# FNet and MLP mixer on one core: the first tile's mean in halves, the second tile loaded behind the third chunk of weights, and the products of the first two tiles alternated

## The chip, the core and the metric

The kernel runs on one core of a Trainium2 chip. A core has five engines with a queue of instructions each: TensorE (matrix products; PE in the profile, its weight loads PEld), VectorE (DVE), ScalarE (ACT), GpSimd (POOL) and SyncE (SP, which here issues transfers). They run side by side and wait for one another by semaphores. The metric is the device time of one execution in microseconds; the figure for a kernel is the median of several executions without the profiler.

## The reference

`x` is 2048 tokens of 512 features, float32. The reference normalizes, mixes by a discrete Fourier transform over features and tokens, and gates the result by an MLP:

```python
xn = layernorm(x)                         # over the features, eps 1e-5, no scale or shift
a  = xn @ dft_hid_re.T                    # 2048 x 512
b  = xn @ dft_hid_im.T
s  = dft_seq_re @ a - dft_seq_im @ b      # real part of the transform over the tokens
h  = gelu(layernorm(xn) @ w1 + b1)        # 512 -> 1792, tanh form
g  = silu(h @ w2 + b2)                    # 1792 -> 512
out = x + s * g
```

## The kernel before

Every operand of a product is kept as two float32 parts, a rounded one (high, made by ScalarE) and what is left (low, made by VectorE as the difference), and a product is three products of TensorE: high by high, low by high, high by low. Below, `hl2` means: high part of the tile, low part of the weights, chunk 2 of the 512 features.

The stages follow one another on TensorE: the transform over the features (`pd`, lines 361 and 376, then `q` for the last tokens), the MLP (`h`, `m`), and the transform over the tokens (`px`, `pz`, `pw`). The tokens go in 16 tiles of 128. The first four tiles are loaded as rows, centred and transposed by TensorE; the other tiles come from a transposed copy of `x` in memory and are centred with a row of means. The factors 1/sqrt(variance) are applied later, where a product leaves PSUM.

The order of the instructions is written out by hand: each engine runs its instructions in the order in which the program's lines issue them, and waits where an operand is not there yet. The change touches the head of the kernel, the first 25 us or so. Its pieces:

- `x_load(i)` (line 211) and `load_w` (line 221) issue transfers on SP's queue, 256 KB each: one tile of `x`, or one of the eight chunks of feature weights `wt[m, k]` (`m` 0 the real part, 1 the imaginary, `k` the chunk of 128 features). Chunk `n` here is `m * 4 + k`.
- `first_mean(i)` (line 249), `first_centre(i)` (line 256), `first_var(i)` (line 262): mean, centring and variance of a row tile. Tile 0's mean and variance come from VectorE's `bn_stats` (line 118) and `bn_aggr` (line 119), the others' from sums that ScalarE accumulates as it copies or squares (lines 252 and 263).
- `first_transpose(i)` (line 265): four transposes by TensorE, then the split into high (ScalarE, line 64) and low part (VectorE, line 65). Tile 0 goes in two halves.
- `round_w(n)` and `rest_w(n)` (lines 297 and 302): high part of a chunk by ScalarE (line 300), low part by VectorE (line 83).
- `first_mm` (line 366): tile 0's products with both halves of the weights, tile 1's transposes among them. `dft_mm(i, m)` (line 355): twelve products of tile `i`; it can issue something (`mid`) before its n-th product.
- `idle_mm` (line 192): products of zeros at the start and before the first real product.
- `m_pack` and `m_turn` (lines 309 and 314): means of tiles 4 to 7 packed as columns, transposed by TensorE, stored, and loaded back by SP as a row over all partitions. `xt_centre` and `xt_make` then centre and split these tiles.

The order of the head, as written in the kernel before:

```python
x_load(0); load_w(0, 0); load_w(0, 1); load_w(1, 0); x_load(1); load_w(1, 1); x_load(2); x_load(3)
```

so x0, chunks 0 to 5, x1, chunks 6 and 7, x2, x3. Chunk 0 is split, tile 0 transposed, chunks 1 to 5 split, tile 1 centred, chunks 6 and 7 split. The products: all twelve of tile 0 with the real part, six with the imaginary one, tile 1's transposes, the other six, then tile 1 with the real part (tile 2's transposes among them), tile 1 with the imaginary part, the turn of the row of means, tile 2.

Of the kernel before, what the change touches and what calls it, by code (L numbers as in the profile page):

```python
# [8 lines left out]
F32 = mybir.dt.float32  # L9
# [3 lines left out]
AF = mybir.ActivationFunctionType  # L13
ALU = mybir.AluOpType

P = 128
# [6 lines left out]
def fnet_mixer_kernel(ctx: ExitStack, tc: tile.TileContext, x, xT, ct, wt, w1, w2, b1, b2, out):  # L23
    nc = tc.nc
    S, D = x.shape
    assert D == W
    NS = S // P
    NK = D // P
# [8 lines left out]
    small = ctx.enter_context(tc.tile_pool(name="small", bufs=4))  # L37
# [18 lines left out]
    def bank(name):  # L56
        return psum.tile([P, W], F32, tag="ps", name=name)

    def room(name):
        return lp.tile([P, 2, W], F32, tag="l", name=name)  # L60
# [41 lines left out]
    mv1 = consts.tile([P, NS, 2], F32, name="mv1")  # L102
# [13 lines left out]
    def stats(mv, t, i):  # L116
        st = small.tile([P, 6], F32, tag="st", name="st")
        nc.vector.bn_stats(st, t)
        nc.vector.bn_aggr(mv[:, i, :], st)
# [21 lines left out]
    def first_factors():  # L141
        v = small.tile([P, 2 * HB], F32, tag="v", name="v")
        inner(v[:, :HB], mv1[:, :HB, 1], 1.0)
        outer(v[:, HB:], mv1[:, :HB, 1], 1.0)
        rsqrt(rr[:, :2 * HB], v, 2 * HB)
        nc.vector.tensor_scalar(nr1, rr[:, :HB], -1.0, None, op0=ALU.mult)
# [45 lines left out]
    def idle_mm(n):  # L192
        for q in range(n):
            nc.tensor.matmul(idle_ps, idle[:, :P], idle, start=True, stop=True)  # L194
# [3 lines left out]
    xs = {}  # L198
# [9 lines left out]
    def parts(i):  # L208
        return 1 if i else 2

    def x_load(i):
        if i % 2 == 0:
            x_two[i // 2] = guest(f"x{i}")
        xs[i] = x_two[i // 2][:, i % 2, :]
        nc.sync.dma_start(out=xs[i], in_=x[tok(i) * P:(tok(i) + 1) * P, :])

    raw_w = []
    room_w = {}


    def load_w(m, k2):
        t = room(f"rw{m}{k2}")
        for k in (2 * k2, 2 * k2 + 1):
            nc.sync.dma_start(out=t[:, k % 2, :], in_=wt[m, k])
            raw_w.append(t[:, k % 2, :])
        room_w[m, k2] = t

    warm = small.tile([P, 1], F32, tag="warm", name="warm")
    nc.vector.memset(warm, 0.0)
# [1 line left out]
    nc.scalar.dma_start(out=touched[:P // 8].rearrange("p (n w) -> p n w", w=4),  # L231
                        in_=wt[:, :, 0:P:8, 0:4].rearrange("m k p w -> p (m k) w"))
    x_load(0)
    for k2 in range(NK // 2):
        load_w(0, k2)
    load_w(1, 0)
    x_load(1)
    load_w(1, 1)
    x_load(2)
    x_load(3)  # L240
    a_d = [dram.tile([2, P, D], F32, name=f"a_d{i}") for i in range(NS // 2)]
# [4 lines left out]
    xt = {}  # L246
    xc = {}

    def first_mean(i):
        xc[i] = plain(f"xc{i}")  # L250
        if i:
            nc.scalar.activation(xc[i], xs[i], AF.Copy, scale=1.0 / D, accum_out=mv1[:, i, 0:1])
        else:
            stats(mv1, xs[i], i)

    def first_centre(i):
        n = D // parts(i)
        for q in range(parts(i)):
            nc.vector.tensor_scalar(xc[i][:, q * n:(q + 1) * n], xs[i][:, q * n:(q + 1) * n], mv1[:, i, 0:1], None,
                                    op0=ALU.subtract)  # L260

    def first_var(i):
        nc.scalar.activation(xs[i], xc[i], AF.Square, scale=D ** -0.5, accum_out=mv1[:, i, 1:2])

    def first_transpose(i):
        t = operand(f"xt{i}")
        hi, lo = t[:, 0, :], t[:, 1, :]
        n = D // parts(i)
        for q in range(parts(i)):
            pt = bank(f"pt{i}{q}")  # L270
            for k in range(NK // parts(i)):
                nc.tensor.transpose(pt[:, k * P:(k + 1) * P], xc[i][:, q * n + k * P:q * n + (k + 1) * P], ident)
            split_into(hi[:, q * n:(q + 1) * n], lo[:, q * n:(q + 1) * n], pt[:, :n])
        for k in range(NK):
            xt[i, k] = (hi[:, k * P:(k + 1) * P], lo[:, k * P:(k + 1) * P])
# [19 lines left out]
    weights = [None] * (2 * NK)  # L295

    def round_w(n):
        t = operand(f"W{n}")
        weights[n] = (t[:, 0, :], t[:, 1, :])
        nc.scalar.activation(weights[n][0], raw_w[n], AF.Copy)  # L300

    def rest_w(n):
        rest(weights[n], raw_w[n])
# [10 lines left out]
    def m_turn():  # L314
        ps = bank("rpm1")
        nc.tensor.transpose(ps[:NC, :P], row_st["m1"], ident)
        sb = small.tile([NC, P], F32, tag="rt", bufs=1, name="rtm1")
        nc.scalar.activation(sb, ps[:NC, :P], AF.Copy)
        d = dram.tile([COPIES, W], F32, name="rdm1")
        nc.scalar.dma_start(out=d.rearrange("r (b p) -> b r p", p=P),  # L320
                            in_=sb[:, None, :].broadcast_to([NC, COPIES, P]))
        t = guest("rowm1_0")
        n = P // COPIES
        for r in range(COPIES):
            nc.sync.dma_start(out=t[r * n:(r + 1) * n, 0, :], in_=d[r].partition_broadcast(n))
        mrow[1] = t[:, 0, :]
# [9 lines left out]
    def act_stats(i):  # L336
        if not squares:
            squares.append(guest("squares"))
        t, = squares
        c = i % NC  # L340
        nc.scalar.activation(t[:, 0, :], xs[i], AF.Copy, scale=-1.0 / D, accum_out=nm[:, NC + c:NC + c + 1])
        nc.scalar.activation(t[:, 1, :], xs[i], AF.Square, bias=nm[:, NC + c:NC + c + 1], accum_out=sq[:, c:c + 1])
# [9 lines left out]

    dacc, e_two = {}, {}

    def dft_mm(i, m, mid=None, at=2 * NK):
        acc = bank(f"pd{i}_{m}")
        terms = [(0, 0, k) for k in range(NK)] + [(1, 0, k) for k in range(NK)] + [(0, 1, k) for k in range(NK)]
        for n, (px, pw, k) in enumerate(terms):
            if mid and n == at:
                mid()  # L360
            nc.tensor.matmul(acc, xt[i, k][px], weights[m * NK + k][pw], start=n == 0, stop=n == len(terms) - 1)  # L361
        dacc[i, m] = acc

    def first_mm(mid):
        for m in range(2):
            dacc[0, m] = bank(f"pd0_{m}")
        seen = [0, 0]
        for m, what in ((0, "hh0 hl0 lh0 hh1 lh1 hl1 hh2 lh2 hl2 hh3 lh3 hl3"), (1, "hh0 lh0 hh1 lh1 hl0 hl1"),  # L370
                        (None, ""), (1, "hh2 lh2 hh3 lh3 hl2 hl3")):
            if m is None:
                mid()
            for o in what.split():
                px, pw, k = "hl".index(o[0]), "hl".index(o[1]), int(o[2])
                nc.tensor.matmul(dacc[0, m], xt[0, k][px], weights[m * NK + k][pw], start=seen[m] == 0,  # L376
                                 stop=seen[m] == 3 * NK - 1)
                seen[m] += 1

    def dft_at(i, m):  # L380
        return (b_d if m else a_d)[tok(i) // 2][tok(i) % 2]
# [14 lines left out]
    def store():  # L396
        dst, e = stores.pop(0)
        nc.sync.dma_start(out=dst, in_=e)

    first_mean(0)  # L400
    first_centre(0)
    round_w(0)
    rest_w(0)
    first_transpose(0)
    for n in (1, 2, 3, 4, 5):
        round_w(n)
        rest_w(n)
    first_mean(1)
    first_centre(1)
    for n in (6, 7):  # L410
        round_w(n)
        rest_w(n)
    for q in range(NC):
        x_load(NC + q)
    xt_load(1)
    for q in (12, 13, 8, 9):
        x_load(q)

    idle_mm(1)
    first_mm(lambda: first_transpose(1))  # L420
    first_mean(2)
    first_var(1)
    first_centre(2)
    stats(mv1, xs[NC], NC)
    stats(mv1, xs[NC + 1], NC + 1)
    dft_mm(1, 0, mid=lambda: first_transpose(2))
    first_mean(3)
    first_var(2)
    first_centre(3)
    first_var(3)  # L430
    stats(mv1, xs[NC + 2], NC + 2)
    stats(mv1, xs[NC + 3], NC + 3)
    m_pack()
    dft_mm(1, 1)
    m_turn()
    for q in (14, 15, 10, 11):
        x_load(q)
    for q in (12, 13):
        act_stats(q)
    first_factors()  # L440
    for q in (8, 9):
        stats(mv1, xs[q], q)
    dft_mm(2, 0, mid=lambda: first_transpose(3))
    dft_out(0, 0)
    dft_out(0, 1)
    dft_out(1, 0)
# [137 lines left out]
    for i in range(3, HB):  # L584
        if i == 3:
            xt_prepare(1)
            for q in (14, 15):
                act_stats(q)
            for q in (10, 11):
                stats(mv1, xs[q], q)  # L590
            neg_means(2)
            neg_means(0)
        if i == 4:
            second_factors()
        if i == 5:
            a_sums()
            last_factors()
        if i == 6:
            for b in (2, 3):
                for k2 in range(2):  # L600
                    y_centre(b, k2)
        if i == 7:
            y_scale(0, 2)
            y_round("11", 1)
            y_scale(1, 2)
            y_round("21", 1)
            y_rest("11", 1)
            y_rest("21", 1)
        dft_mm(i, 0, mid=turn_r if i == 5 else None, at=2)
        if i == 5:  # L610
            rrow = [None] * 2 + row_load("R", 2, 2)
        dft_out(i - 1, 1)
        if i == 4:
            row_st["n"] = nm
            rows_turn("n")
            mrow[2], mrow[3] = row_load("n", 2)
        dft_mm(i, 1)
        dft_out(i, 0)
# [640 lines left out]
```

## Time and profile before

| what | value |
|---|---|
| median of 3 executions | 667.26 us (667.09 to 667.33) |
| profiled execution: whole time | 668.27 us |
| profiled execution: span from first to last instruction | 666.5 us |
| TensorE busy | 661.4 us, 99% of the span, 2926 products and transposes |
| VectorE busy | 542.5 us, 81% |
| ScalarE busy | 358.3 us, 54% |
| granted TensorE clock | 1.000 over the span |

The profile is one execution with the profiler on. A row of its timeline gives the start and the duration in microseconds from the start of the span, the engine, the line of the kernel, the operation, the names written and read (`pd<-W,xt`), the shapes, and how many like instructions are merged (`x8`); the brackets at the end give how long the engine had stood idle before and what ended that wait. `DMA` there means a transfer that landed. The chain that ended last follows the work back from the last instruction, each time to what released it. Names: `x` row tiles, `xc` centred, `pt` transposed in PSUM, `xt` split; `rw` raw chunks of weights, `W` split; `pd` products.

### The profile page before, as it was taken

To read this page: it belongs to the slowest core of one execution; us is meant where nothing else is said; L and a number is where in the kernel's file an instruction comes from. 1 tells how busy PE (TensorE), PEld (TensorE's weight loads), DVE (VectorE), ACT (ScalarE), POOL (GpSimd) and SP (SyncE) were. 2 spreads that over 40 slices of the span, in tenths; PEclk is the share of its full clock that TensorE was granted. 3 is DMA by queue.
4 is the path that set the end of the run, shared out by engine and by line. 5 is a ranking of instruction groups with operands and counts; after the bars stand their busy time and mean duration, and the time that the engine had idled before them with its cause. 6 is when DMAs were issued, how large, how long until landed. Compare 5 with 4: busy or idle time off the path is not lost.

```text
span 666.5 us, 8218 instructions
## 1 busy us (share of the span) xinstructions
PE 661.4 (99%) x2926; PEld 544.6 (82%) x2926; DVE 542.5 (81%) x590; ACT 358.3 (54%) x407; POOL 50.7 (8%) x84
## 2 busy tenths in 40 slices
PE   9999999999999999999999999999999999999997
PEld 5888888888888888888888888888888888888886
DVE  6889878867777866988979998739878299998986
ACT  6836647554456655555455544446545454746540
POOL 0002000321212100000000000000000001210100
PEclk9999999999999999999999999999999999999999
DMA  8689360787889999797799996416545448996983
GB/s 312 221 287 236 107 241 4 299 312 288 328 307 351 416 415 357 270 392 275 297 389 409 358 326 236 158 40 212 184 152 139 128 125 263 304 258 243 309 255 137
DMA packets 70821, 172.29 MB, mean 258 GB/s; under 512 B 6864, under 2 KB 21756, under 8 KB 70780
## 3 DMA queue, kind: packets, MB, share of 16 engines
q1 hardware_dynamic: 58528, 131.88, 56.2%
q0 software_dynamic: 12032, 39.86, 19.1%
q8 instruction: 23, 0.38, 0.2%
q14 instruction: 18, 0.15, 0.1%
q10 hardware_dynamic: 220, 0.02, 0.0%
HBM read 121.38 MB, written 50.35 MB: 258 GB/s over the span
## 4 chain that ended last, share of the span: by engine, by line
PE 99%; DVE 0%; issue 0%
PE pz L873 20%; PE px L873 18%; PE ma L873 11%; PE hy L688 11%; PE mb L873 9%; PE pd L361 6%; PE hz L688 6%; PE pw L873 5%; PE qy L568 3%; PE hx L688 3%; PE px L1194 2%; PE pw L1194 2%; PE qz L568 2%; PE pd L376 1%; PE qx L568 1%; PE idle_ps L194 1%
## 5 line engine op out<-in xcount | busy, mean ns | idle before, releaser
L979 DVE TENSOR_TENSOR c<-c,c 128x1024 f32<-128x1024 f32 x32 | 38.9, 1217 | 4.8 <-DMA c<-ct 4.8
L83 DVE TENSOR_TENSOR w1l<-w1r,w1h 128x1792 fp32r<-128x1792 f32 x7 | 14.2, 2026 | 21.6 <-ACT w1h L475 21.6
L693 ACT ACTIVATE hc<-hc,b_t 128x1024 f32<-128x1024 f32 (+1 forms) x18 | 17.3, 960 | 25.2 <-DVE hc L733 22.6
L65 DVE TENSOR_TENSOR R_b1l<-c,R_b1h 128x1024 fp32r<-128x1024 f32 x16 | 19.5, 1221 | 13.0 <-ACT R_b1h L64 9.7
L64 ACT ACTIVATE R_s3h<-c 128x1024 fp32r<-128x1024 f32 x16 | 17.0, 1061 | 23.7 <-DVE c L979 12.3
L873 PE MATMUL pw<-R_s1h,L 128*128 128x512 f32 x96 | 29.7, 389 | 0.0
L64 ACT ACTIVATE R_b2h<-c 128x1024 fp32r<-128x1024 f32 x16 | 16.9, 1058 | 21.2 <-DVE c L984 16.7
L65 DVE TENSOR_TENSOR R_s2l<-c,R_s2h 128x1024 fp32r<-128x1024 f32 x16 | 19.5, 1221 | 8.6 <-PE pz L873 8.6
L64 ACT ACTIVATE R_s2h<-c 128x1024 fp32r<-128x1024 f32 x16 | 17.0, 1061 | 16.7 <-PE px L873 9.3
L65 DVE TENSOR_TENSOR R_s3l<-c,R_s3h 128x1024 fp32r<-128x1024 f32 x16 | 19.5, 1218 | 4.0 <-PE pz L873 4.0
L64 ACT ACTIVATE R_s1h<-c 128x1024 fp32r<-128x1024 f32 x16 | 16.4, 1050 | 11.4 <-DVE c L990 11.4
L987 POOL DMA_DIRECT2D c<-ct x8 | 7.0, 873 | 200.6 <-DVE c L984 162.9
L64 ACT ACTIVATE R_b1h<-c 128x1024 fp32r<-128x1024 f32 x16 | 16.7, 1053 | 9.5 <-PE px L873 4.4
L64 ACT ACTIVATE R_a1h<-c 128x1024 fp32r<-128x1024 f32 x16 | 16.9, 1054 | 8.9 <-PE pz L873 7.2
L873 PEld LDWEIGHTS pw<-R_s1h,L 128*128 128x128 f32 x96 | 18.0, 188 | 3.7
L65 DVE TENSOR_TENSOR R_b2l<-c,R_b2h 128x1024 fp32r<-128x1024 f32 x16 | 19.4, 1218 | 1.5 <-PE px L873 1.5
L65 DVE TENSOR_TENSOR R_a1l<-c,R_a1h 128x1024 fp32r<-128x1024 f32 x16 | 19.5, 1219 | 1.3 <-PE px L873 1.1
L65 DVE TENSOR_TENSOR R_s4l<-c,R_s4h 128x1024 fp32r<-128x1024 f32 x16 | 19.5, 1217 | 0.7 <-PE px L873 0.7
L984 DVE TENSOR_TENSOR c<-c,c 128x1024 f32<-128x1024 f32 x16 | 19.6, 1223 | 0.4
L64 ACT ACTIVATE R_s4h<-c 128x1024 fp32r<-128x1024 f32 x16 | 16.8, 1051 | 5.3 <-PE pz L873 5.0
L65 DVE TENSOR_TENSOR R_s1l<-c,R_s1h 128x1024 fp32r<-128x1024 f32 x16 | 18.8, 1219 | 0.4 <-ACT R_s1h L64 0.2
L64 ACT ACTIVATE w2h<-w 128x1024 fp32r<-128x1024 f32 (+1 forms) x14 | 13.2, 944 | 10.6 <-DVE w L801 3.9
(954 smaller groups left out, 2226.4 us busy)
## 6 DMA issues: line engine op xcount, KB each, us to landing
c<-ct SPq DMA_DIRECT2D x68, 512.0 KB, 5.1
m<-h_d SPq DMA_DIRECT2D x48, 512.0 KB, 6.8
h_d<-ht POOLq DMA_DIRECT2D x21, 512.0 KB, 5.9
s_d<-sa SPq DMA_DIRECT2D x32, 256.0 KB, 4.0
la<-s_d SPq DMA_DIRECT2D x32, 256.0 KB, 6.6
h_d<-hc POOLq DMA_DIRECT2D x13, 512.0 KB, 3.8
x<-x SPq DMA_DIRECT2D x16, 256.0 KB, 5.4
sa<-a_d SPq DMA_DIRECT2D x8, 512.0 KB, 5.7
```

Of the source, the lines that this page charges most:

```text
L64: nc.scalar.activation(hi, src, AF.Copy)
L65: nc.vector.tensor_sub(lo, src, hi.bitcast(F32))
L83: nc.vector.tensor_sub(hi_lo[1], src, hi_lo[0].bitcast(F32))
L361: nc.tensor.matmul(acc, xt[i, k][px], weights[m * NK + k][pw], start=n == 0, stop=n == len(terms) - 1)
L568: nc.tensor.matmul(qx[key, c], a, w, start=p in (1, 5, 2) and n == 0, stop=p in (2, 3, 4) and n == len(terms) - 1, skip_group_check=True)
L688: nc.tensor.matmul(acc[:, tau, :], w[:, W1_AT[p], k * P:(k + 1) * P], r[:, k, :], start=p in (1, 5, 2) and i == 0, stop=p in (2, 3, 4) and ...
L693: nc.scalar.activation(dst, src, AF.Gelu_apprx_tanh, bias=b1_t[:, row:row + 1])
L873: nc.tensor.matmul(acc[k][:, tau, :], a, c[:, tau, :], start=first and i == 0, stop=last and i == len(terms) - 1, skip_group_check=True)
L979: nc.vector.tensor_sub(t, t, raw)
L984: nc.vector.tensor_add(raw, raw, t)
L987: nc.gpsimd.dma_start(out=t, in_=ct[1, 1, n], accum_op=ALU.add)
L1194: nc.tensor.matmul(acc[KEY[name]][k][:, tau, cols], a[k], c[:, tau, cols], start=False, stop=last and u == us[-1] and i == 2, skip_group_c ...
```

## The change

The first tile's mean is taken in halves: ScalarE sums the first 256 columns while it copies them (with the factor 1/512), VectorE sums the other 256 with a reduction and scales the sum; centring subtracts both half means in one instruction. Tile 0's variance is no more a by-product and is made by ScalarE, in the same way as the other tiles', and a small addition puts the mean together for later use. On SP's queue x1 stands behind chunk 2 instead of chunk 5. ScalarE and VectorE split chunks 1 and 2, then make tile 1's mean and centre it, then split chunks 3 and 4; chunks 5 to 7 come behind tile 1's transposes. The products of tiles 0 and 1 are issued in turns. The turn of the row of means, and what is issued with it, moves two products further, into tile 2's.

```diff
-    for k2 in range(NK // 2):
-        load_w(0, k2)
-    load_w(1, 0)
+    for n in range(3):
+        load_w(n)
     x_load(1)
-    load_w(1, 1)
+    for n in range(3, 2 * NK):
+        load_w(n)
     x_load(2)
     x_load(3)
...
+    half_means = [small.tile([P, 1], F32, tag=f"hm{q}", bufs=1, name=f"hm{q}") for q in range(2)]
...
         if i:
             nc.scalar.activation(xc[i], xs[i], AF.Copy, scale=1.0 / D, accum_out=mv1[:, i, 0:1])
-        else:
-            stats(mv1, xs[i], i)
+            return
+        n = D // 2
+        nc.scalar.activation(xc[i][:, :n], xs[i][:, :n], AF.Copy, scale=1.0 / D, accum_out=half_means[0])
+        nc.vector.reduce_sum(half_means[1], xs[i][:, n:], axis=mybir.AxisListType.X)
+        nc.vector.tensor_scalar(half_means[1], half_means[1], 1.0 / D, None, op0=ALU.mult)
...
+        for q in range(2):
+            nc.vector.tensor_scalar(xc[i][:, q * n:(q + 1) * n], xs[i][:, q * n:(q + 1) * n], half_means[0],
+                                    half_means[1], op0=ALU.subtract, op1=ALU.subtract)
...
     first_mean(0)
     first_centre(0)
-    round_w(0)
-    rest_w(0)
+    make_w(0)
     first_transpose(0)
-    for n in (1, 2, 3, 4, 5):
-        round_w(n)
-        rest_w(n)
+    idle_mm(1)
+    make_w(1, 2)
     first_mean(1)
     first_centre(1)
-    for n in (6, 7):
-        round_w(n)
-        rest_w(n)
+    make_w(3, 4)
+    first_mm(0, 0, "hh0 hl0 lh0 hh1 lh1 hl1 hh2 lh2 hl2 hh3 lh3")
+    first_transpose(1)
+    first_mm(0, 0, "hl3")
+    make_w(5, 6, 7)
...
-    idle_mm(1)
-    first_mm(lambda: first_transpose(1))
+    first_mm(0, 1, "hh0 lh0 hl0")
+    first_mm(1, 0, "hh0 hl0 hh1 hl1 hh2 hl2 hh3 hl3 lh0 lh1 lh2 lh3")
     first_mean(2)
+    first_centre(2)
+    first_var(0)
     first_var(1)
-    first_centre(2)
     stats(mv1, xs[NC], NC)
     stats(mv1, xs[NC + 1], NC + 1)
-    dft_mm(1, 0, mid=lambda: first_transpose(2))
+    first_mm(0, 1, "hh1 lh1 hh2 lh2 hh3 lh3")
+    first_transpose(2)
+    first_mm(0, 1, "hl1 hl2 hl3")
     first_mean(3)
+    first_centre(3)
     first_var(2)
-    first_centre(3)
     first_var(3)
...
     m_pack()
-    dft_mm(1, 1)
-    m_turn()
-    for q in (14, 15, 10, 11):
-        x_load(q)
-    for q in (12, 13):
-        act_stats(q)
-    first_factors()
-    for q in (8, 9):
-        stats(mv1, xs[q], q)
-    dft_mm(2, 0, mid=lambda: first_transpose(3))
+    nc.vector.tensor_add(mv1[:, 0, 0:1], *half_means)
+    first_mm(1, 1, "hh0 hh1 hh2 hh3 lh0 lh1 lh2 lh3 hl0 hl1 hl2 hl3")
+
+    def means_out():
+        m_turn()
+        for q in (14, 15, 10, 11):
+            x_load(q)
+        for q in (12, 13):
+            act_stats(q)
+        first_factors()
+        for q in (8, 9):
+            stats(mv1, xs[q], q)
+
+    dft_mm(2, 0, {2: means_out, 8: lambda: first_transpose(3)})
```

`load_w(n)` now issues one chunk, `make_w` splits chunks, `first_mm(i, m, what)` issues the listed products, and `dft_mm` takes a table of what to issue before which product.

More of the change, by code (lines that the diff above doesn't have):

```diff
@@ L218, in fnet_mixer_kernel, with load_w @@
     room_w = {}
[L221 to L226, printed above, removed]
+    def load_w(n):
+        m, k = divmod(n, NK)
+        if k % 2 == 0:
+            room_w[m, k // 2] = room(f"rw{m}{k // 2}")
+        raw_w.append(room_w[m, k // 2][:, k % 2, :])
+        nc.sync.dma_start(out=raw_w[n], in_=wt[m, k])
     warm = small.tile([P, 1], F32, tag="warm", name="warm")
@@ L252, in first_mean @@
             nc.scalar.activation(xc[i], xs[i], AF.Copy, scale=1.0 / D, accum_out=mv1[:, i, 0:1])
-        else:
-            stats(mv1, xs[i], i)
-    def first_centre(i):
[L257 to L260, printed above, removed]
+            return
[3 more added lines that the diff above has]
+        nc.vector.tensor_scalar(half_means[1], half_means[1], 1.0 / D, None, op0=ALU.mult)
+    def first_centre(i):
+        if i:
+            nc.vector.tensor_scalar(xc[i], xs[i], mv1[:, i, 0:1], None, op0=ALU.subtract)
+            return
+        n = D // 2
+        for q in range(2):
+            nc.vector.tensor_scalar(xc[i][:, q * n:(q + 1) * n], xs[i][:, q * n:(q + 1) * n], half_means[0],
+                                    half_means[1], op0=ALU.subtract, op1=ALU.subtract)
     def first_var(i):
@@ L353, in fnet_mixer_kernel, with dft_mm @@
     dacc, e_two = {}, {}
-    def dft_mm(i, m, mid=None, at=2 * NK):
+    def dft_mm(i, m, mids={}):
         acc = bank(f"pd{i}_{m}")
@@ L358, in dft_mm, with first_mm @@
         for n, (px, pw, k) in enumerate(terms):
-            if mid and n == at:
-                mid()
+            if n in mids:
+                mids[n]()
             nc.tensor.matmul(acc, xt[i, k][px], weights[m * NK + k][pw], start=n == 0, stop=n == len(terms) - 1)
         dacc[i, m] = acc
[L366 to L378, printed above, removed]
+    seen = {}
+    def first_mm(i, m, what):
+        if (i, m) not in seen:
+            seen[i, m] = 0
+            dacc[i, m] = bank(f"pd{i}_{m}")
+        for o in what.split():
+            px, pw, k = "hl".index(o[0]), "hl".index(o[1]), int(o[2])
+            nc.tensor.matmul(dacc[i, m], xt[i, k][px], weights[m * NK + k][pw], start=seen[i, m] == 0,
+                             stop=seen[i, m] == 3 * NK - 1)
+            seen[i, m] += 1
     def dft_at(i, m):
@@ L398, in store, with make_w @@
         nc.sync.dma_start(out=dst, in_=e)
+    def make_w(*ns):
+        for n in ns:
+            round_w(n)
+            rest_w(n)
     first_mean(0)
     first_centre(0)
-    round_w(0)
-    rest_w(0)
+    make_w(0)
     first_transpose(0)
-    for n in (1, 2, 3, 4, 5):
-        round_w(n)
-        rest_w(n)
+    idle_mm(1)
+    make_w(1, 2)
     first_mean(1)
     first_centre(1)
-    for n in (6, 7):
-        round_w(n)
-        rest_w(n)
+    make_w(3, 4)
[3 more added lines that the diff above has]
+    make_w(5, 6, 7)
     for q in range(NC):
@@ L608, in fnet_mixer_kernel @@
             y_rest("21", 1)
-        dft_mm(i, 0, mid=turn_r if i == 5 else None, at=2)
+        dft_mm(i, 0, {2: turn_r} if i == 5 else {})
         if i == 5:
```

## The prediction

> **What bounds the kernel now.** I read the page's busy times and the chain that ended last first, then the timeline of the first 33 us engine by engine, in windows of 0.2 us where single instructions matter, then the list of waits.
>
> ```profile
> PE 661.4 (99%) x2926; PEld 544.6 (82%) x2926; DVE 542.5 (81%) x590; ACT 358.3 (54%) x407; POOL 50.7 (8%) x84
> PE 99%; DVE 0%; issue 0%
> 21.99 11.82 PE pd L361 x52
> ```
>
> TensorE is the bound, and the chain of waits is TensorE from end to end: 52 products in 11.82 us, 0.227 us for one. The change neither adds nor removes a product of TensorE, so only waits of TensorE can move the end, and the edit touches only those of the head. TensorE's timeline there:
>
> ```profile
> 1.20 3.59 PE L194 MATMUL idle_ps<-idle 128*128 128x512 bf16 x8 [1.20 <-DVE warm L229]
> 4.15 0.63 PE L194 MATMUL idle_ps<-idle 128*128 128x512 bf16 x1
> 4.76 1.09 PE L272 MATMUL pt<-ident,xc 128*128 128x128 f32 x4
> 5.00 0.85 PE L272 MATMUL pt<-ident,xc 128*128 128x128 f32 x3
> 5.21 0.64 PE L272 MATMUL pt<-ident,xc 128*128 128x128 f32 x2
> 5.64 0.63 PE L194 MATMUL idle_ps<-idle 128*128 128x512 bf16 x1
> 6.93 0.53 PE L376 MATMUL pd<-W,xt 128*128 128x512 f32 x1
> 7.47 0.30 PEld L376 LDWEIGHTS pd<-W,xt 128*128 128x128 f32 x2 [0.64 <-ACT W L300]
> 8.20 0.30 PEld L376 LDWEIGHTS pd<-W,xt 128*128 128x128 f32 x2 [0.43 <-DVE W L83]
> 8.54 0.64 PE L376 MATMUL pd<-W,xt 128*128 128x512 f32 x2
> 9.02 0.62 PE L376 MATMUL pd<-W,xt 128*128 128x512 f32 x2
> 9.25 0.85 PE L376 MATMUL pd<-W,xt 128*128 128x512 f32 x3
> 11.09 0.40 PE L376 MATMUL pd<-W,xt 128*128 128x512 f32 x1
> 11.47 0.42 PEld L272 LDWEIGHTS pt<-ident,xc 128*128 128x128 f32 x4 [0.40 <-DVE xc L259]
> 15.19 0.60 PE L272 MATMUL pt<-ident,xc 128*128 128x128 f32 x4
> 15.54 3.92 PE L361 MATMUL pd<-W,xt 128*128 128x512 f32 x16
> ```
>
> A printed duration holds the pipeline's depth; what counts is start to start. The eight idle products start 0.42 us apart ((4.15 - 1.20)/7) and the transposes 0.21, where products of the same 512 columns later start 0.23 apart: TensorE is at about half speed until some 7.2 us. From there three waits are left: for W1's high part (the third product started at 6.93, so it is through by 7.35; the next goes at 7.47, and its weight load adds 0.11), about 0.23; for W1's low part, 8.20, where the next product follows 0.34 later instead of 0.23, together about 0.27; and for tile 1's centred rows, 11.47 instead of 11.09 + 0.23 = 11.32, about 0.16. After that no wait of TensorE appears. All three together are 0.66 us. What feeds them:
>
> ```profile
> 3.31 0.69 DVE L118 BATCH_NORM_STATS2 st<-x 128x6 f32<-128x512 f32 x1 [2.17 <-DMA x<-x]
> 4.04 0.18 DVE L119 BATCH_NORM_AGGREGATE mv<-st 128x2 f32<-128x6 f32 x1
> 4.26 0.62 DVE L259 TENSOR_SCALAR xc<-x,mv 128x256 f32<-128x256 f32 x2
> 4.13 0.63 ACT L300 ACTIVATE W<-rw 128x512 fp32r<-128x512 f32 x1 [1.89 <-DMA rw<-wt]
> 5.46 0.38 ACT L64 ACTIVATE xt<-pt 128x256 fp32r<-128x256 f32 x1 [0.70 <-PE pt L272]
> 5.87 0.85 DVE L65 TENSOR_TENSOR xt<-pt,xt 128x256 fp32r<-128x256 f32 x2 [0.39 <-ACT xt L64]
> 6.79 0.63 ACT L300 ACTIVATE W<-rw 128x512 fp32r<-128x512 f32 x1 [0.53 <-DMA rw<-wt]
> 8.12 0.63 ACT L300 ACTIVATE W<-rw 128x512 fp32r<-128x512 f32 x1
> 8.80 0.63 ACT L300 ACTIVATE W<-rw 128x512 fp32r<-128x512 f32 x1
> 9.48 0.63 ACT L300 ACTIVATE W<-rw 128x512 fp32r<-128x512 f32 x1
> 10.18 0.63 ACT L252 ACTIVATE xc<-x 128x512 f32<-128x512 f32 x1
> 10.71 0.19 ACT L252 ACTIVATION_READ_ACCUMULATOR xc<-x 128x1 f32 x1
> 10.93 0.49 DVE L259 TENSOR_SCALAR xc<-x,mv 128x512 f32<-128x512 f32 x1
> 11.49 0.63 ACT L300 ACTIVATE W<-rw 128x512 fp32r<-128x512 f32 x1
> 15.82 0.60 ACT L64 ACTIVATE xt<-pt 128x512 fp32r<-128x512 f32 x1 [1.83 <-PE pt L272]
> ```
>
> ScalarE starts each rounding as its chunk lands: W0 4.13, then a hole, W1 6.79, and W7, seven transfers behind W1, at 11.49 ((11.49 - 6.79)/7 = 0.67 us a transfer, tile 1 among them at 10.18). W1's landing, 2.66 us after W0's, ends the half-speed stage.
>
> **The change, part by part.**
>
> *Tile 0's mean in halves.* Off VectorE go 0.69 + 0.18 us; on it come a half reduction and a tiny multiply. No reduction is in the trace; its bounds are 0.31 (half of the centring pair's 0.62) and 0.69 (the whole 512 columns), and I take 0.43, half of the pair at 5.87, the nearest 256-column row of an operation that runs at a 512-column rate of 0.69. The multiply costs at most the 0.18 of the aggregate. Centring then begins at 3.31 + 0.43 + 0.18 + two hand-overs of 0.03 = 3.98 instead of 4.26; with the upper bound at 4.24. ScalarE's half mean, between 0.38 (256 columns out of PSUM) and 0.63, plus 0.19, is done by 3.31 + 0.82 = 4.13 at the worst, just when W0 is due. [...]
>
> What does it bring? TensorE is in its idle products until 4.15 + 0.42 = 4.58, so the transposes begin at 4.58, not 4.76. Four at 0.21, the idle product 0.42, three products 0.43 each: through at 7.15 instead of 7.35. The next product still waits for W1, 6.79 + 0.63 = 7.42, and starts at 7.47. Gain at the end: 0. If the mean came late instead, these 0.3 us are the cover.
>
> *Tile 1 in the queue's fifth place, third chunk in front.* The same transfers in the same number, so I leave the landing times to the places: x1 lands when W3 did, just ahead of 8.12, W3 at 8.80, W4 at 9.48, W5 at 10.18, W6, W7 unchanged. No issue is added; SP waits per place as before. ScalarE's order becomes W1, W2, x1's mean at 8.12, W3 at 8.80. So W3's high part is ready at 9.43 instead of 8.75, and the product that wants it, whose slot is 9.25, loads at 9.48 and runs from 9.59: a new wait of 0.34 us, by the pattern of the one at 8.20. This is the price of the swap. ScalarE itself has room, since the mean (0.63, its read-out overlapping) ends as W3 lands.
>
> *Tile 1's transposes before the last product of chunk 3.* x1's mean is read out at 8.12 + (10.71 + 0.19 - 10.18 = 0.72) = 8.84, centred by 8.87 + 0.49 = 9.36; the transposes' turn is 9.59 + 2 x 0.23 = 10.05. The wait at 11.47 is gone: -0.16, and with the smoother restart after them (next products at +0.35 and +0.32 as at 15.19 and 15.54) about -0.2.
>
> *Products alternated.* After the transposes four products need no tile 1 (last one of chunk 3, three of chunk 4): the first of tile 1 has its turn at 10.05 + 0.35 + 0.32 + 3 x 0.23 = 11.41; the transposes end by 10.65 (0.60), ScalarE copies by 11.28, loaded at 11.33, running at 11.44: +0.03. Twelve products of tile 1 then use chunks 0 to 3 and run to 14.17. Meanwhile ScalarE rounds W5, W6, W7 from 11.3 to 13.2; first wanted 14.17, 14.6, 15.1: cover 1 us and more, against nothing before (W6 and W7 were wanted as they were made). Tile 2's mean follows to 13.9, centring on VectorE, behind W7's low part (0.69 at the 512-column rate, to about 14.0), ends 14.5; its transposes come at 15.53.
>
> *Tile 0's variance by ScalarE.* One square, 0.63 + 0.19, and a 0.18 add on VectorE. ScalarE had 1.83 us of idle time before 15.82 and the new one sits in the same place, after tile 2's mean; it ends by 15.1, tile 2's copy comes at 16.15: hidden.
>
> *Row of means turned two products later.*
>
> ```profile
> 19.20 0.17 DVE L166 COPY rsm<-mv 128x4 f32<-128x4 f32 x1
> 19.43 0.27 PE L316 MATMUL rpm<-ident,rsm 128*4 128x128 f32 x1
> 26.08 2.36 DVE L287 TENSOR_TENSOR xT<-xT,rowm 128x1024 f32<-128x1024 f32 x2 [1.17 <-DMA rowm<-rdm]
> 29.58 1.22 DVE L65 TENSOR_TENSOR xt_1l<-xT,xt_1h 128x1024 fp32r<-128x1024 f32 x1
> 32.29 0.62 PE L361 MATMUL pd<-W,xt_1l 128*128 128x512 f32 x2
> SPq L325 <- DMA rdm<-rtm: 8.1, 1, 8.1
> ```
>
> Tile 2's transposes come after 33 products instead of 32, at 15.53 against 15.19, so the packing slips 0.34 to 19.54 and is done at 19.71; the turn, 17 products behind those transposes instead of 16, is due at 15.53 + (19.43 - 15.19) + 0.23 = 20.00: 0.24 us of cover. Behind the turn everything slips by 0.57: the store, SP's four row loads and the four loads of x queued behind them (SP sat there 8.1 us anyway), the centring at 26.08, and the last operand of it, ready at 29.58 + 1.22 = 30.80, at 31.37. It is wanted at 32.29 + 0.11: 1.03 us of cover.
>
> **Sum.** 0 (start) + 0.34 (chunk 3) - 0.20 (tile 1's centring) + 0.03 = +0.17; by the other count, tile 2's transposes at 15.53 against 15.19 + 0.23 for the one product more, +0.11. I take +0.1 us, within 0.2%, which is about what a measurement of this kernel can tell from no change (1.3 us). The profiled execution took 668.27, 1.0 more than the median; the forecast is 668.4 against it, and 667.26 + 0.1 = 667.4 against the median.
>
> **Rivals.** (1) *The waits of the head vanish.* If W1 lands in step (0.67 after W0), all three waits of before go from the kernel after, with 0.2 of the earlier start: at most -0.86, 666.4. For it: tile 1's twelve products give TensorE work that needs no further chunk. Against: the hole sits ahead of the swapped places, and chunk 3 is put off. It would still be within 0.2%. 0.18.
>
> (2) *Slower: x1 is the late transfer.* One transfer of this head took 2.66 us where the others take 0.67. Should x1, now right behind the hole, do the same, W3 and all behind come 2.0 us later and TensorE has nothing beyond chunk 2: +0.1 + 2.0 = 669.4. It decides from a delay of about 1.2 us. Against: in its old place it landed in step, 0.70 after W5. 0.04.
>
> (3) *Half speed for longer.* TensorE's products ran 0.42 apart up to 6.93 and 0.23 apart from 8.54, with the granted clock at 1.00 throughout. If the switch came after 10.5, as it could with the gaps of the new order, the eight products from 7.47 would take 0.43 each, and the transposes start at 7.47 + 8 x 0.43 = 10.9 instead of 10.05: +0.85 on the forecast, 668.2. Against: TensorE's first 6 us keep the same work, only 0.2 earlier. [...] 0.04.
>
> The forecast, +0.1 with 0.3 either way, has 0.72; 0.02 is left for the moved turn running out of its cover. Its own range is 667.1 to 667.7. The range for 8 in 10 goes from 666.6, which takes most of rival 1, to 668.2, rival 3. Faster by over 0.2% (below 665.9) needs more than all waits listed: 0.03. Slower by over 0.2% (above 668.6) is rival 2 and little else: 0.04. Within: 0.93.
>
> **What would show it.** Transposes of tile 0 at 4.58; a wait for W1 near 7.4 that is longer than 0.64; a weight load at 9.48 waiting for ScalarE's W; tile 1's transposes near 10.05 without a wait; tile 2's near 15.5; the turn near 20.0; no wait before 32.4. Wrong if x1 or W3 lands out of step, if the reduction takes over 0.7, or if a wait shows between 20 and 33 us.

## The result, and the profile after

The changed kernel takes 671.19 us (median of 6 executions, 671.02 to 671.32), the kernel before, measured beside it, 667.3 us (667.09 to 667.68). The ratio is 1.0056 [1.0045, 1.0067]: 3.9 us slower. The prediction was 667.4 us, in a range from 666.6 to 668.2, with 0.93 on no measurable change. It was wrong, and the place of the loss is one that it did not look at.

The page of the kernel after, its span, its busy times and the chain that ended last (the profiled execution took 671.32 us):

```profile
span 669.5 us, 8225 instructions
PE 664.5 (99%) x2926; PEld 544.7 (81%) x2926; DVE 542.0 (81%) x591; ACT 359.3 (54%) x411; POOL 50.8 (8%) x84
PE 99%; DVE 0%; issue 0%
```

The same number of products keeps TensorE busy for 3.1 us more (664.5 against 661.4), and the chain is still all TensorE. So it is not a wait: somewhere the products themselves take longer. That can't be read from busy shares; it is read from how far apart products start, stage by stage.

First the head, which the edit touches. TensorE's timeline of the kernel after:

```profile
4.82 1.09 PE L280 MATMUL pt<-ident,xc 128*128 128x128 f32 x4
5.96 3.35 PE L381 MATMUL pd<-W,xt 128*128 128x512 f32 x11
9.15 0.60 PE L280 MATMUL pt<-ident,xc 128*128 128x128 f32 x4
14.64 0.60 PE L280 MATMUL pt<-ident,xc 128*128 128x128 f32 x4
18.98 0.27 PE L324 MATMUL rpm<-ident,rsm 128*4 128x128 f32 x1
30.00 0.39 PE L369 MATMUL pd<-W,xt_0h 128*128 128x512 f32 x1
```

and that of the kernel before, at the last of these places:

```profile
30.93 0.62 PE L361 MATMUL pd<-W,xt_0h 128*128 128x512 f32 x2
```

Tile 4's first product starts at 30.00 instead of 30.93: the head of this execution was 0.9 us *faster*. Now the chain that ended last, where the transform over the features (`qy`) gives over to the MLP's first layer (`hx`, `hy`, `hz`: 588 products, w1 against y), inside that layer, and at the last of its products. Before (start, duration, products):

```profile
89.85 1.36 PE qy L568 x6
91.21 1.36 PE hy L688 x6
...
151.05 5.44 PE hy L688 x24
...
227.21 2.72 PE hy L688 x12
229.93 13.60 PE ma L873 x60
```

After:

```profile
79.85 10.43 PE qy L585 x46
90.28 1.40 PE hy L705 x6
...
151.88 5.60 PE hy L705 x24
...
230.14 2.80 PE hy L705 x12
232.94 13.63 PE ma L890 x60
```

At the layer's first products the kernel after is 0.93 us ahead (90.28 against 91.21), at its last ones 2.93 us behind (230.14 against 227.21). The layer lost 3.9 us, and the pieces show how: 24 products take 5.60 us where they took 5.44, 233.3 ns for one instead of 226.7. 588 products at 6.67 ns more are 3.92 us. On both sides of the layer nothing differs (`ma`: 13.60 and 13.63 for 60). The table of stretches says the same by counts; its columns are the stretch, its length, the busy time and count of TensorE, its weight loads, VectorE, ScalarE and GpSimd, then the granted clock, the share of the transfers and GB/s. Before, in the transform over the features, in the layer, and behind it:

```profile
30.00:90.00 60.00, 60.00 (x267) 49.47 (x266) 54.60 (x81) 31.76 (x49) 4.29 (x5) 1.00 0.78 235
125.00:175.00 50.00, 50.00 (x222) 41.39 (x222) 35.78 (x40) 24.48 (x24) 11.17 (x21) 1.00 0.86 312
240.00:340.00 100.00, 100.00 (x443) 82.81 (x442) 80.97 (x81) 54.76 (x56) 1.06 (x2) 1.00 0.90 332
```

After:

```profile
30.00:90.00 60.00, 60.00 (x267) 49.49 (x266) 54.61 (x81) 31.40 (x45) 4.29 (x5) 1.00 0.77 233
125.00:175.00 50.00, 50.00 (x216) 40.30 (x215) 35.81 (x40) 23.09 (x23) 10.66 (x20) 1.00 0.82 299
240.00:340.00 100.00, 100.00 (x442) 82.80 (x442) 80.48 (x81) 52.06 (x54) 1.07 (x2) 1.00 0.89 327
```

TensorE is 100% busy at a granted clock of 1.00 in all six rows, and yet in the middle ones it makes 222 products in 50 us before and 216 after. The transfers move less there, not more (299 GB/s against 312). No instruction of the layer was edited. What differs is where its operands lie: the edit adds two tiles of one column, `half_means`, to the pool `small`. In the compiled programs each takes 32 bytes of every partition, and pools lie one behind the other, so all that is stacked behind `small` moves by 64 bytes. The split w1 (pool `wp`) is there; y (pool `op`) lies ahead and stays. These addresses are the program's; the trace does not hold them.

### The profile page after: what moved, and what is told of

Same layout as the page of the kernel before. It is cut to its first block, busy times and chain, and to the rows that moved or that the text cites. A ratio compares the mean times of both kernels' runs of the same rounds, so it can differ in the third digit from the quotient of the medians.

```text
span 669.5 us, 8225 instructions
## 1 busy us (share of the span) xinstructions
PE 664.5 (99%) x2926; PEld 544.7 (81%) x2926; DVE 542.0 (81%) x591; ACT 359.3 (54%) x411; POOL 50.8 (8%) x84
## 4 chain that ended last, share of the span: by engine, by line
PE 99%; DVE 0%; issue 0%
PE pz L890 19%; PE px L890 18%; PE hy L705 12%; PE ma L890 11%; PE mb L890 9%; PE hz L705 6%; PE pd L369 5%; PE pw L890 5%; PE qy L585 3%; PE hx L705 3%; PE pd L381 2%; PE px L1211 2%; PE pw L1211 2%; PE qz L585 2%; PE qx L585 1%; PE idle_ps L194 1%
```

## The experiments

In what follows, *distance* is the address of w1, the stationary operand, less that of y, the moving one, modulo 256 bytes where nothing else is said. All slices of y and of a w1 tile used in a product start at multiples of 512 bytes from their tile's start, so the pair has one distance for the whole layer. Before it is 0, after it is 64.

**One: the pad alone.** The kernel before, with two tiles that nothing uses:

```diff
+    pads = [small.tile([P, 1], F32, tag=f"pad{q}", bufs=1, name=f"pad{q}") for q in range(2)]
```

> The kernel before with two more one-column tiles in the pool of small tiles, never used: 64 bytes a partition, so that every pool reserved behind it, the one with the split w1 among them, starts 64 bytes later. No instruction changes. Address theory (the stationary operand w1 starts 64 bytes past a multiple of 128 bytes, and each of the 588 products with it costs 6.7 ns more): the products of the MLP's first layer go from 0.2267 to 0.2333 us apart and the time from 667.3 to 671.2 us. Rival (the slower stage comes from the new order of the head, its transfers or its waits): 667.3 us, products 0.2267 apart.

Measured: 671.56 us (671.22 to 671.77), ratio to the kernel before 1.0062 [1.0048, 1.0075]. The chain, in the layer:

```profile
143.78 5.60 PE hy L689 x24
```

Not one instruction was changed, and the whole loss is there, 233.3 ns a product.

**Two: the change without its new tiles.** The half means go into two columns of a tile that exists already:

```diff
-    half_means = [small.tile([P, 1], F32, tag=f"hm{q}", bufs=1, name=f"hm{q}") for q in range(2)]
+    half_means = [nr1[:, q:q + 1] for q in range(2)]
```

> The changed kernel with the two half means kept in two columns of nr1, a tile that is there anyway and is written only later, so that no address moves; every instruction stays. Address theory: the first layer's products are 0.2267 us apart again, 3.9 us go, and what the head gained in the profile (0.9 us) is left over: 666.4 us, or 667.2 if the head's gain was only the landing of the second chunk in that one execution. Rival (order of the head): 671.2 us.

Measured: 667.33 us (667.2 to 667.91, 11 executions) against 667.47 for the kernel before, ratio 1.0 [0.9991, 1.0009]. The layer:

```profile
141.86 5.44 PE hy L705 x24
```

All of the edit's work is in this kernel: mean in halves, order of transfers, order of products. It takes the same time as before, to 0.1%. So the loss belongs to the two tiles and to nothing else, and the rest of the change is worth nothing measurable.

**Three and four: w1 moved by itself.** In the kernel before (three) and in the kernel after (four), an unused tile of 64 bytes in the pool `wr`, just ahead of `wp`: pools of the head stay where they were, and w1 moves by 64 bytes more. That makes the distance 64 in three and 128 in four.

```diff
+    wr.tile([P, 16], F32, tag="pad", name="wpad")
```

> The kernel before with an unused tile of 64 bytes a partition in the pool of the raw w1, so that only this pool and the ones stacked on it while the MLP's first layer runs (the split w1, one pool of loads) move by 64 bytes; the pools of the head stay. Address theory, with w1 as the operand that matters: 671.2 us, as with all pools moved. If the moved pools of the head or of the small tiles matter instead: 667.3 us.

> The changed kernel with the same unused tile, so that the split w1 starts 128 bytes later than in the kernel before and the other pools stay 64 bytes off. Address theory: 667.3 us or, with the head's gain, 666.4 us; products of the first layer 0.2267 us apart. Rival (order of the head, or any move of w1): 671.2 us.

Measured: three 671.77 us (671.64 to 671.81), ratio 1.0065 [1.0051, 1.0079]; four 671.32 us (670.84 to 671.63), 1.0058 [1.0044, 1.0071]. The layer of three and of four:

```profile
143.79 5.60 PE hy L689 x24
```

```profile
143.64 5.57 PE hy L706 x24
```

Three shows that it is w1's place (or that of the raw w1 and of the pool of loads, which move along), and not the small tiles of the head. Four refutes the rule that I had formed first, that a multiple of 128 bytes is enough: at 128 it is 232.4 ns, hardly better than 233.3.

**Five to eight: one distance per buffer.** To try several distances in one execution, the four buffers of w1 were given places of their own, with pads between them; in the eighth, all of `op` (y and most other operands) was moved by 64 bytes too. Each has one time. The edit of five (the others differ in `W1_PADS`; eight has the pool `shift` of experiment nine besides):

```diff
+    W1_PADS = [0, 32, 32, 32]
-        w1_op[j] = [wp.tile([P, 7, 2 * P], F32R, tag="w", name=f"w1{v}{j}") for v in "hl"]
+        w1_op[j] = []
+        for i, v in enumerate("hl"):
+            q = (2 * j + i) % 4
+            if j < 2 and W1_PADS[q]:
+                wp.tile([P, W1_PADS[q] // 4], F32, tag=f"pad{q}", name=f"pad{q}")
+            w1_op[j].append(wp.tile([P, 7, 2 * P], F32R, tag=f"w{q}", name=f"w1{v}{j}"))
-    wp = early.enter_context(tc.tile_pool(name="wp", bufs=4, reuse_waits="tile"))
+    wp = early.enter_context(tc.tile_pool(name="wp", bufs=1, reuse_waits="tile"))
```

> The kernel before with its four buffers of split w1 moved by 0, 32, 64 and 96 bytes against their old places (even chunks: high part in the first, low part in the second; odd chunks: third and fourth). What is read is the distance from one product's start to the next, by the buffer of the later product's stationary operand. Both address theories: 0.2267 us at 0, 0.2333 at 64. If only a start off a multiple of 64 or 128 bytes cost, 32 and 96 would be slow too and all alike; if the distance to the moving operand counts, 32 and 96 may lie in between.

> The same with 128, 192, 256 and 320 bytes. The first address theory (multiples of 128 bytes) wants 128 and 256 at 0.2267 us and 192 and 320 at 0.2333; the run with w1 moved by 128 bytes already speaks against it (0.232). If the place counts modulo 256 bytes, 256 is at 0.2267; if modulo 512, all four are slow.

> The same with 384, 448, 512 and 768 bytes. Place modulo 512 bytes: 512 at 0.2267 us, the others slow. Modulo 256: 512 and 768 at 0.2267. If only the old place itself is fast, all are slow.

> The kernel before with the pool of all other operands (y, the weights and tiles of every other stage) moved by 64 bytes, and the four w1 buffers by 64, 128, 512 and 576 bytes against their old places, that is by 0, 64, 448 and 512 against y. Relative theory (what counts is the distance of the stationary from the moving operand, modulo 512): buffers 1 and 4 at 0.2267 us, 2 and 3 slow, and all other stages stay at 0.2267, since there both operands moved together. Absolute theory (the stationary operand's own place): buffer 3 fast, 1 and 4 slow, and the other stages slow as well, some 1,900 products by 6.7 ns or 13 us more.

Measured, beside 667.75 for the kernel before: 671.05, 670.4, 670.36 and 669.55 us; mean of the layer 232.4, 231.8, 231.2 and 230.1 ns a product. One piece of the chain of each, five to eight:

```profile
143.63 5.58 PE hy L694 x24
```

```profile
143.02 5.57 PE hy L694 x24
```

```profile
143.30 5.56 PE hy L694 x24
```

```profile
142.92 5.51 PE hy L696 x24
```

As a table of distances these four missed: I had looked for a clean 226.7 at the buffers with distance 0. From one product of such a buffer to the next it is 231.7 in five and 228.4 in seven, although both operands lie as in the kernel before. In eight the products of the buffers at distance 0, expected fast, are even the slowest (231.1 on average, 229.2 at 64 and 228.9 at 448, modulo 512). With mixed distances the products of one buffer don't stand for themselves, and the numbers per buffer can't be read as a rule. Eight did settle one thing. Nearly every operand of the kernel lay 64 bytes further there, and a stage behind the layer kept its pace (443 products in 100 us, as before). Eight, then before:

```profile
500.00:600.00 100.00, 100.00 (x443) 82.84 (x442) 83.03 (x73) 52.20 (x53) 11.79 (x12) 1.00 0.75 202
```

```profile
500.00:600.00 100.00, 100.00 (x443) 82.81 (x442) 84.04 (x75) 52.02 (x53) 11.79 (x12) 1.00 0.75 203
```

A multiple of 64 bytes as such is no fault, then; what is left to try is how two operands lie to each other.

**Nine to twelve: one distance at a time.** Nine moves everything by 64 bytes, w1 and y alike; ten moves w1 alone by 512 bytes, eleven by 256, twelve adds one unused small tile (32 bytes) instead of two.

```diff
+    shift = ctx.enter_context(tc.tile_pool(name="shift", bufs=1))           # nine
+    shift.tile([P, 16], F32, tag="shift", name="shift")                     # nine
+    wr.tile([P, 128], F32, tag="pad", name="wpad")                          # ten
+    wr.tile([P, 64], F32, tag="pad", name="wpad")                           # eleven
+    pads = [small.tile([P, 1], F32, tag=f"pad{q}", bufs=1, name=f"pad{q}") for q in range(1)]  # twelve
```

> The kernel before with every tile moved by 64 bytes, w1 as well as y: an unused tile of 64 bytes in front of all pools. w1 stands where it stands in the changed kernel, but its distance to y is the old one. Relative theory (only the distance of the stationary from the moving operand, modulo 512 bytes, counts): all products 0.2267 us apart, 667.4 us. Absolute theory (w1's own place): first layer 0.2333 us, 671.4 us.

> The kernel before with all four w1 buffers moved by 512 bytes, y in place. Relative theory with a period of 512 bytes: 0.2267 us, the time of before. If the distance counts as such, without a period: slow, 0.232 us or so and 670 to 671 us.

> The kernel before with all four w1 buffers moved by 256 bytes. Period of 512: slow, 0.229 us or more (about 1 to 4 us on the whole), Period of 256: 0.2267 us and the time of before.

> The kernel before with one more one-column tile among the small tiles (32 bytes a partition), which moves w1 by 32 bytes, y in place. Relative theory: slow as well, between 0.229 and 0.233 us a product, 1.5 to 4 us more. If only 64 bytes and up count: the time of before.

Measured: nine 667.59 us (667.12 to 667.89, 10 executions), ratio 1.0003 [0.9993, 1.0012]; ten, eleven and twelve, one time each beside 667.43 for the kernel before, 668.87, 668.18 and 671.21. The layer of nine, ten, eleven and twelve:

```profile
141.86 5.44 PE hy L690 x24
```

```profile
143.48 5.44 PE hy L689 x24
```

```profile
142.79 5.44 PE hy L689 x24
```

```profile
143.41 5.60 PE hy L689 x24
```

In nine, w1 starts at byte 188608 of the partition, the very place that it has in the kernel after, and the layer is as fast as before: the distance counts, not the place. 256 and 512 bytes are as good as 0, so the view that the period is 512 fell with eleven, and 128 is too short a one by experiment four: 256 fits all runs with one distance. Seven, read again with eleven in mind, also answers, if 256 is the period, what three left open: there the raw w1 keeps its old place and the pool of loads lies 768 bytes, three times 256, further, so only the places of w1's own buffers are left for its 4.5 ns more a product. No run moves y apart from the other tiles of `op`; that the distance to y counts, and not to another tile there, is argued from y being the other operand of these products. Ten and eleven are a little long as wholes for another reason: in their single profiles the layer starts at 91.64 and 90.95, and in ten TensorE waited 0.8 us for `q`, in the stage ahead of it. All runs with one distance, with the time from the first product of the layer to its last (24 products of `ma` lie between):

```
run                        w1 - y, bytes mod 512   ns a product   layer, us   whole, us
before                       0                     226.7          138.49      667.3
two  (change, no new tiles)  0                     226.7          138.49      667.33
nine (all + 64)              0                     226.7          138.49      667.59
ten  (w1 + 512)              0                     226.7          138.49      668.87
eleven (w1 + 256)          256                     226.7          138.49      668.18
twelve (w1 + 32)            32                     233.3          142.41      671.21
after                       64                     233.3          142.44      671.19
one  (before, pad)          64                     233.3          142.44      671.56
three (before, w1 + 64)     64                     233.3          142.44      671.77
four (after, w1 + 64 more) 128                     232.4          141.92      671.32
```

The layer is the same to 0.03 us within each group. Not tried: distances between 128 and 256 alone, and the other stages' operands at other distances.

## Why the prediction was wrong

**The step that failed** is the one in the first part: "The change neither adds nor removes a product of TensorE, so only waits of TensorE can move the end, and the edit touches only those of the head." The first half is true and the conclusion does not follow: the length of a product was taken as fixed. The sum had no term for the two new tiles, though the diff shows them; that term is 588 x 6.67 ns = +3.92 us, and it is the whole result (667.3 + 3.9 = 671.2). None of the three rivals named it, and the range did not reach it. The result lies above even rival 2 (669.4), but has nothing to do with it: no transfer was late.

The head, point by point. ScalarE and VectorE of the kernel after:

```profile
3.54 0.42 ACT L257 ACTIVATE xc<-x 128x256 f32<-128x256 f32 x1 [1.30 <-DMA x<-x]
4.30 0.63 ACT L308 ACTIVATE W<-rw 128x512 fp32r<-128x512 f32 x1 [0.25 <-DMA rw<-wt]
6.23 1.15 ACT L308 ACTIVATE W<-rw 128x512 fp32r<-128x512 f32 x2
7.27 0.62 ACT L254 ACTIVATE xc<-x 128x512 f32<-128x512 f32 x1
7.89 1.14 ACT L308 ACTIVATE W<-rw 128x512 fp32r<-128x512 f32 x2
```

```profile
3.54 0.42 DVE L258 TENSOR_REDUCE hm<-x 128x1 f32<-128x256 f32 x1 [2.40 <-DMA x<-x]
4.00 0.15 DVE L259 TENSOR_SCALAR hm<-hm 128x1 f32<-128x1 f32 x1
4.26 0.74 DVE L267 TENSOR_SCALAR xc<-x,hm,hm 128x256 f32<-128x256 f32 x2
28.69 1.22 DVE L65 TENSOR_TENSOR xt_1l<-xT,xt_1h 128x1024 fp32r<-128x1024 f32 x1
```

Two rows of TensorE's weight loads there:

```profile
6.91 0.30 PEld L381 LDWEIGHTS pd<-W,xt 128*128 128x128 f32 x2 [0.19 <-ACT W L308]
7.63 0.53 PEld L381 LDWEIGHTS pd<-W,xt 128*128 128x128 f32 x3 [0.43 <-DVE W L83]
```

- *Mean in halves.* The half reduction takes 0.42 us (taken 0.43), as much as one of the two subtractions of its size at 5.87 in the profile of before (0.85 for both); the multiply takes 0.15 (at most 0.18), ScalarE's half 0.42. Centring begins 0.72 after tile 0 landed (3.54 to 4.26; predicted 0.67), and the transposes 1.28 after, against 4.76 - 3.31 = 1.45 before: 0.17 sooner, predicted 0.18 (4.58 for 4.76). Tile 0 landed 0.23 later in this execution, so the start itself is at 4.82.
- *The wait for W1, and the new wait for W3.* The new wait is not there, in this profile or in the two others with the new order of the head (experiments two and four). Of the wait for W1 a part is left. The hole between the first two chunks, which the profile of before shows at 6.79, is not in this one: ScalarE takes W1 at 6.23, right behind tile 0's copies, without a wait for a transfer, then W2, tile 1's mean at 7.27 and W3 at 7.89 in one run. The load of W1's high part still waits 0.19 us (0.64 before), and that of its low part 0.43, as long as before, so of the three waits the 0.27 for the low part stays. Rival 1's condition, W1 without the hole, came true, but not all three waits went with it. I had read the hole of a single profile as a feature of the kernel: in the ten other profiles with the old order ScalarE takes W1 between 5.69 and 6.37, and in none does it wait for it.
- *The half speed.* It, too, was taken from a single profile. Before, the third product starts 0.43 us behind the second (6.50, 6.93); after, 0.23 (6.53, 6.76). The rows print a granted clock of 1.00 throughout, but the traces also hold the moments at which the clock changes: full speed begins at 7.2 us before and at 6.5 after, and between 4.1 and 7.2 in the fourteen profiles of this case, the one of before being the latest. The prediction let W1's landing end the half speed; in experiment nine full speed begins at 4.7, and ScalarE takes W1 at 5.98, so that is not shown to be its cause. Rival 3, half speed for longer, did not come; that the gaps of the new order could put the switch off to 10.5 was an assumption of that rival that no run shows.
- *Tile 1's centring.* Its transposes start at 9.15 and TensorE waits for nothing there: the 0.16 is gone as predicted.
- *Products alternated, variance by ScalarE.* One weight load waits 0.19 us for tile 1's copy, at 10.44, and no product starts late for it; both cost nothing that can be seen.
- *The turn of the row of means.* It comes 4.34 us behind tile 2's transposes (14.64 to 18.98; predicted 15.53 to 20.00, 4.47) and does not start late. The last operand behind it, `xt_1l`, is ready at 28.69 + 1.22 = 29.91. It is wanted 1.36 us behind the product that started at 30.00 (32.29 - 30.93 before), at 31.36: cover 1.45, predicted 1.03.

So the head is 0.9 us ahead in this pair of profiles. That is close to rival 1's "at most -0.86", but by chance: from tile 0's first product to the first one with W2 it takes 2.01 us (5.96 to 7.97) instead of 2.65 (5.89 to 8.54), and the shorter half speed has its part in that. It is not the change that made it so. The layer's first product started between 90.02 and 91.64 in the eleven profiles of kernels with the old order of the head (median 90.42; 91.05 in the one of before), and at 90.02, 90.11 and 90.49 in the three with the new one. The timed comparison is experiment two, and there the new head is worth nothing measurable, -0.6 to +0.6 us by its interval. The forecast for the edit's work itself, +0.1 us and no measurable change, stands by that run, but not for its reasons: the +0.34 for W3 did not come, and the terms can't be told apart by it.

## What to carry to other kernels

A new tile, however small and however idle, is a change of address for all that is allocated behind it, and belongs in the sum; put a few columns into a tile that exists, or pad a pool, so that the stationary and the moving float32 operand of a long run of products keep a distance that was seen to be fast (here 0 and 256 bytes modulo 512). When a change is slower with the same instructions and no new wait, compare products per microsecond stage by stage, since a busy share of 99% hides 3% of a stage. To test such a suspicion, add an unused tile to the old kernel: in experiment one that changed no instruction and showed the whole loss.

## What the runs showed of the hardware

That 128x128 float32 weights and a 128x512 float32 moving operand (declared `float32r` in the kernel) give 226.7 ns a product when their addresses differ by 0 or 256 bytes modulo 512, 233.3 ns at 32 or 64 and 232.4 ns at 128, was not expected. The weight loads themselves did not grow. Tiles of the layer by name (shortest, median and longest in ns, then when). Before:

```profile
L688 PE MATMUL hy<-yt_0h,w1h x38: 389/389/389, 112.8 to 211.4; 128*128 128x512 f32 x38
L688 PEld LDWEIGHTS hy<-yt_0h,w1h x38: 187/188/188, 112.6 to 211.2; 128*128 128x128 f32 x38
```

After:

```profile
L705 PE MATMUL hy<-yt_0h,w1h x38: 393/396/398, 112.5 to 214.0; 128*128 128x512 f32 x38
L705 PEld LDWEIGHTS hy<-yt_0h,w1h x38: 188/188/188, 112.3 to 213.8; 128*128 128x128 f32 x38
```

A product's printed time grows from 389 to 396 ns, as its spacing does; a load stays at 188. The loads overlap the running products (by the printed times each of the layer's 588 starts while the product ahead of it runs, in both profiles). Experiments one and nine show an effect of the distance: 233.3 ns a product at 64 bytes, 226.7 at 0. What happens inside is shown by no run and stays open, as does why 128 bytes (232.4) differs a little from 32 and 64 (233.3).
